# Matmuls of zeros at the start, hi and lo ahead of the additions in two MLPs, an earlier bias sum and a halved last eviction

## The chip, the cores and the metric

The kernel runs on one core of a Trainium2 chip. The metric is the device time of one execution in microseconds (us); of several runs the median counts. PE is the matmul engine, PEld its weight loads, DVE, ACT and POOL are the vector, scalar and GpSimd engines, SP issues most transfers.

## What is computed

```python
scores = (1.0 / S) * np.matmul(z, z.transpose(0, 2, 1))
attn = np.maximum(scores, 0.0) ** 2
x = u * np.matmul(attn, v)
h = x @ moe_w_in
x = np.maximum(0.01 * h, h) @ moe_w_out
r = np.maximum(x @ moe2_w_in, 0.0)
out = (s * (r * r) + b) @ moe2_w_out
```

There are 2 batches of S = 3008 tokens, 256 channels, a `z` of 64 channels, and 2048 hidden channels in each MLP. `u`, `z` and the result are handed over transposed.

## The kernel before

**Precision.** A float32 operand is kept as two parts, `hi` (rounded to the fast fp32r type) and `lo` (what is left of it). A product takes three matmuls: hi with hi, hi weights with lo, lo weights with hi.

**Tokens.** They are cut into 12 tiles, 10 of 512 columns and 2 of 448. The attention goes tile by tile; the MLPs take the tiles in 6 pairs of equal width.

**Attention.** A tile has 12 units, each of two blocks of 128 keys. `scores` (from line 316) issues four matmuls into a PSUM tile `f` (two buffers), then on ACT the activation Relu (L326) and the square (L327), then `hi` on ACT or DVE by turns (L328) and `lo` on DVE (L334). The value matmuls (L349) of a unit follow two units later in PE's order. `split_v` (from line 111) makes hi and lo of three blocks of `v`: hi on ACT (L114), lo on DVE for the first batch (L116). `load_v` fetches `v` three groups ahead. What happens in which unit is put down in `hooks` by `at(step, fn)`; `sv` runs `split_v` of group g at step `g * VG // 2` with `VG = 3`, so for g = 0 in step 0, ahead of that step's scores on ACT. Weights, given as float64, are narrowed and split on the side during the attention.

**MLPs.** For a pair of tiles the first product of an MLP is made in 8 blocks of 256 hidden channels (`q` = 0 to 7), each by the scheme with seven products in place of eight on 2 by 2 blocks: 21 matmuls (L415) into three PSUM tiles `x[0]` to `x[2]`. A block has three steps. Step one makes three products, copies `x[0]` to `s1` on ACT (L635) and forms `u2` on DVE (L638). Step two adds a product to `x[0]`, which ACT activates straight into `c11`, and one to `x[1]`; DVE then adds `x[1]` and `x[2]` to `s1` for `c22` (L660, L661). Step three adds A22's product to `x[1]` and S4's to `x[2]`, so it overwrites what L660 and L661 have read; DVE makes `c21` and `c12` (L672, L674).

**Second product.** The results of a block are activated while the next block runs: `activate(0)` for the pair's first tile and `activate(1)` for the second, on ACT (L591 in the first MLP; L593 and the square L604 in the second). `spread` then makes `hi` (L613: on ACT in the first MLP, on DVE in the second) and `lo` (L614, DVE) and puts 12 matmuls of the second product (L434) into a queue. Each step ends with `step_chunk`, which issues 8 of the queue on PE, except the step numbered 4, where nothing is taken. Each engine works through its own list strictly in the order in which the program issues it. In the last block of a pair, and in blocks 0 and 6, operands of the next pair or of this one are split besides (L407 on ACT, L408 on DVE).

**Bias.** `b` times the column sums of the last weights is needed for the last evictions. `bias_columns`, called in block 4 of the second pair of the first MLP, adds the two halves of the sum on DVE (L469) and multiplies by ones on PE (L472).

**End.** An accumulator of the second MLP is evicted by ACT (L451, channels 0 to 127) or DVE (L455, channels 128 to 255), and SP sends it out.

Of the kernel before, what the change touches and what calls it, by code (L numbers as in the profile page):

```python
# [10 lines left out]
F32 = mybir.dt.float32  # L11
F32R = mybir.dt.float32r
I32 = mybir.dt.int32
U32 = mybir.dt.uint32
AF = mybir.ActivationFunctionType
ALU = mybir.AluOpType
P = 128
# [3 lines left out]
QT = 512  # L21

VG = 3
# [5 lines left out]
def relu2_attention__then__leaky_mlp__then__relu2_mlp_kernel(  # L29
# [25 lines left out]
    nc = tc.nc  # L55
# [45 lines left out]
    def load_v(bb, g):  # L101
        raw = raw_pool.tile([P, 4 * D], F32, tag="raw", name="raw_v")
        r3 = raw.rearrange("p (n d) -> p n d", n=4)
        r0, n = g * VG * P, VG if g < NG - 1 else VG - 1
        nc.sync.dma_start(out=r3[:, 0:n, :], in_=v[bb, r0:r0 + n * P, :].rearrange("(n p) d -> p n d", p=P))
        if n < VG:
            for hh in range(2):
                nc.sync.dma_start(out=r3[hh * HALF:(hh + 1) * HALF, n, :], in_=v[bb, r0 + n * P:S, :])
        raws[bb, g] = raw
# [310 lines left out]
    def queue_second(m, pr, q, ti, hi, lo):  # L420
        t = pr[ti]
        bb, c, n = tiles[t]
        if q == 0:
            acc_t[m, t] = [None, None, None]

        def one(dh, f, i):
            acc = acc_t[m, t]
            if acc[dh] is None:
                acc[dh] = ps_a.tile([P, QT], F32, tag="acc", name=f"acc{dh}")
            w = st["out", m, q // 2]  # L430
            o = f * D + dh * P
            wh, x = ((0, hi), (0, lo), (1, hi))[i]
            last = q == NQ - 1 and f == 1 and i == 2
            nc.tensor.matmul(  # L434
                acc[dh][:, :n], lhsT=w[:, q % 2, wh, o:o + P], rhs=x[:, f, :n],
                start=q == 0 and f == 0 and i == 0, stop=last,
            )
            if m == 1 and pr == pairs[-1] and q % 2 == 1 and ti == dh == f == 1 and i == 2:
                fetch_out(2, q // 2)
            if not last:  # L440
                return
            if dh == 0:
                acc[2] = xio.tile([P, 2, QT], F32, tag="xo", name="x_sb")
            y = acc[2][:, dh, :n]
            if m == 1:
                nc.scalar.copy(out=y, in_=acc[dh][:, :n])
                if dh == 1:
                    nc.sync.dma_start(out=x_d[2, t][:, :, :n], in_=acc[2][:, :, :n])
            else:
                if dh == 0:  # L450
                    nc.scalar.activation(  # L451
                        out=y, in_=acc[0][:, :n], func=AF.Identity, scale=s_sb[:, 0:1], bias=cb[:, 0:1]
                    )
                else:
                    nc.vector.tensor_scalar(  # L455
                        out=y, in0=acc[1][:, :n], scalar1=s_sb[:, 0:1], scalar2=cb[:, 1:2],
                        op0=ALU.mult, op1=ALU.add,
                    )
                nc.sync.dma_start(out=outT[dh * P:(dh + 1) * P, bb * S + c:bb * S + c + n], in_=y)
            if dh == 1:  # L460
                acc_t.pop((m, t))

        for dh in range(2):
            for f in range(2):
                for i in range(3):
                    queue.append(lambda dh=dh, f=f, i=i: one(dh, f, i))

    def bias_columns():
        nc.vector.tensor_tensor(out=wtot, in0=wsum[:, 0:D], in1=wsum[:, D:2 * D], op=ALU.add)  # L469
        f = ps_x.tile([P, QT], F32, tag="x", name="f")  # L470
        for dh in range(2):
            nc.tensor.matmul(f[:, 2 * dh:2 * dh + 2], lhsT=wtot[:, dh * P:(dh + 1) * P], rhs=ones, start=dh == 0, stop=True, skip_group_check=dh > 0)  # L472
        nc.vector.tensor_scalar_mul(out=cb, in0=f[:, 0:4].rearrange("p (d two) -> p d two", two=2)[:, :, 0], scalar1=b_sb[:, 0:1])
# [3 lines left out]
    def at(step, fn):  # L477
        hooks.setdefault(max(step, 0), []).append(fn)

    with tc.manual_schedule():  # L480
# [14 lines left out]
        zrs[2] = load_zk(0, 2)  # L495
        load_v(0, 1)
        load_v(0, 2)
        zr0 = zrs.pop(0)
        make_zk(0, 0, zr0)
        make_zq(0, zr0)  # L500
# [10 lines left out]
        for g in range(NG):  # L511
            def sv(g=g):
                split_v(0, g)
                if g + 3 < NG:
                    load_v(0, g + 3)
            at(g * VG // 2, sv)

        for bb in range(1, B):
            base = bb * TPB * UA
# [96 lines left out]

        def step_chunk():
            nonlocal chunk
            if chunk != 4:
                take(8)  # L620
            chunk += 1

        for m, pr, q in quads:
# [22 lines left out]
            if q == NQ - 1 and ahead:  # L646
                pair_split(*ahead, ORDER[2:3], nc.vector)
            activate(0)
            if before and before[0] == 1:
                activate(1)  # L650
            if q == 4 and ahead:
# [7 lines left out]
            product(x[1], m, pr, q, S3, "T3", False)  # L659
            nc.vector.tensor_tensor(out=c22, in0=x2, in1=s1, op=ALU.add)  # L660
            nc.vector.tensor_tensor(out=c22, in0=x3, in1=c22, op=ALU.add)  # L661
            spread(0)
            if before and before[0] == 2:
                activate(1)
            if q == NQ - 1 and ahead:
# [15 lines left out]
                fetch_in(2, q)  # L681
            step_chunk()
            before = (m, pr, q, cs)
            if m == 1 and pr == pairs[1] and q == 4:
                bias_columns()
        for ti in range(2):
# [39 lines left out]
```

## Time and profile before

| | |
|---|---|
| median of 3 runs | 1515.65 us (1515.13 to 1516.13) |
| the profiled execution's own time | 1514.35 us |
| its span, first to last instruction | 1512.4 us |
| PE busy | 1498.3 us, 99% of the span |
| DVE busy | 1089.8 us, 72% |
| ACT busy | 915.8 us, 61% |
| POOL busy | 191.8 us, 13% |

The rows further down come from the one profiled execution. A time at the start of a row is counted from the span's beginning. Matmuls overlap, so the busy time of one is longer than the distance to the next.

### The profile page before, as it was taken

How to read it: one execution, taken by the hardware profiler on the slowest of the kernel's cores; microseconds unless marked ns; L12 is line 12 of the kernel's file. 1: busy time of each engine (PE TensorE's matmuls, PEld its weight loads, DVE VectorE, ACT ScalarE, POOL GpSimd, SP SyncE). 2: the span in 40 equal slices, each digit the busy share in tenths (PEclk: the TensorE clock that was granted, in tenths of full speed). 3: DMA queues.
4: the chain of work that ended last, by engine and by line, in shares of the span. 5: the costliest groups of instructions: out<-in, count | busy, mean ns of one | idle time of the engine just before them, and what ended most of it. 6: DMA issues, size and time to landing. Idle time of an engine off the chain costs nothing.

```text
span 1512.4 us, 16921 instructions
## 1 busy us (share of the span) xinstructions
PE 1498.3 (99%) x6604; PEld 1237.7 (82%) x6604; DVE 1089.8 (72%) x1369; ACT 915.8 (61%) x1118; POOL 191.8 (13%) x136
## 2 busy tenths in 40 slices
PE   8999999999999999999999999999999999999998
PEld 6888889888888978878889888887777878888776
DVE  6888875899995566566666666667767777777866
ACT  7778878787887645545454545464545545454543
POOL 0332326434431400000000000000000000000000
PEclk9999999999999999999999999999999999999999
DMA  5243434344334620001010102341010101010000
GB/s 156 95 130 130 152 138 126 108 167 153 110 136 158 239 78 17 40 0 53 1 56 1 53 0 105 117 155 42 1 57 1 53 1 56 1 53 1 28 0 28
DMA packets 38831, 113.21 MB, mean 75 GB/s; under 512 B 4064, under 2 KB 13792, under 8 KB 36704
## 3 DMA queue, kind: packets, MB, share of 16 engines
q1 hardware_dynamic: 38528, 111.88, 21.5%
q8 instruction: 51, 0.84, 0.2%
q10 hardware_dynamic: 160, 0.26, 0.1%
q14 instruction: 28, 0.23, 0.0%
q0 software_dynamic: 64, 0.00, 0.0%
HBM read 70.58 MB, written 41.55 MB: 74 GB/s over the span
## 4 chain that ended last, share of the span: by engine, by line
PE 97%; DVE 2%; DMA 0%; ACT 0%; issue 0%; SPq 0%; DVEq 0%
PE acc L434 34%; PE x L415 30%; PE acc L349 25%; PE f L323 8%; DMA raw_v<-in_v_dram 0%; DVE lo L614 0%; DVE lo L334 0%; DVE c L660 0%; DVE hi L332 0%; DVE c L661 0%; ACT a L327 0%; ACT a L326 0%; DVE hi L613 0%; DVE hi L328 0%; SPq L261 0%
## 5 line engine op out<-in xcount | busy, mean ns | idle before, releaser
L415 PE MATMUL x<-top,stat_i 128*128 128x512 f32 (+1 forms) x2016 | 498.6, 386 | 0.8 <-DVE c L660 0.8
L434 PE MATMUL acc<-hi,stat_o 128*128 128x512 f32 (+1 forms) x1536 | 483.7, 386 | 0.0
L415 PEld LDWEIGHTS x<-top,stat_i 128*128 128x128 f32 x2016 | 378.2, 188 | 74.5 <-DVE c L660 1.2
L349 PE MATMUL acc<-hi,stat_v 128*128 128x512 f32 (+1 forms) x1152 | 373.1, 388 | 0.0
L434 PEld LDWEIGHTS acc<-hi,stat_o 128*128 128x128 f32 x1536 | 288.4, 188 | 53.7
L434 PE MATMUL acc<-lo,stat_o 128*128 128x512 f32 (+1 forms) x768 | 301.7, 393 | 0.2
L349 PEld LDWEIGHTS acc<-hi,stat_v 128*128 128x128 f32 x1152 | 217.1, 188 | 42.4 <-DVE hi L328 0.5
L635 ACT COPY a<-x 128x512 f32<-128x512 f32 (+1 forms) x96 | 55.6, 579 | 310.0 <-PE x L415 310.0
L614 DVE TENSOR_TENSOR lo<-c,hi 128x1024 fp32r<-128x1024 f32 (+1 forms) x192 | 230.0, 1198 | 3.3
L334 DVE TENSOR_TENSOR lo<-a,hi 128x1024 fp32r<-128x1024 f32 (+1 forms) x132 | 188.8, 1431 | 56.5 <-ACT hi L328 54.0
L660 DVE TENSOR_TENSOR c<-x,a 128x512 f32<-128x512 f32 (+1 forms) x96 | 65.3, 680 | 221.4 <-PE x L415 221.4
L349 PE MATMUL acc<-lo,stat_v 128*128 128x512 f32 (+1 forms) x552 | 213.8, 387 | 0.7 <-DVE lo L334 0.7
L326 ACT ACTIVATE a<-f 128x1024 f32<-128x1024 f32 (+1 forms) x144 | 145.4, 1010 | 82.3 <-PE f L323 81.1
L434 PEld LDWEIGHTS acc<-lo,stat_o 128*128 128x128 f32 x768 | 144.1, 188 | 44.7 <-DVE lo L614 18.7
L323 PE MATMUL f<-zq,zk 128*128 128x512 f32 (+1 forms) x576 | 156.7, 394 | 7.0 <-DVE zk L272 5.3
L327 ACT ACTIVATE a<-a 128x1024 f32<-128x1024 f32 (+1 forms) x144 | 150.4, 1044 | 4.6
L323 PEld LDWEIGHTS f<-zq,zk 128*128 128x128 f32 x576 | 109.5, 191 | 31.0 <-ACT zq L285 5.3
L349 PEld LDWEIGHTS acc<-lo,stat_v 128*128 128x128 f32 x552 | 104.0, 188 | 22.0 <-DVE lo L334 1.8
L638 DVE TENSOR_TENSOR a<-x,a 128x512 f32<-128x512 f32 (+1 forms) x96 | 65.2, 679 | 68.6 <-PE x L415 67.8
L604 ACT ACTIVATE c<-c 128x1024 f32<-128x1024 f32 (+1 forms) x96 | 100.3, 1045 | 3.0
L613 ACT CAST hi<-c 128x1024 fp32r<-128x1024 f32 (+1 forms) x96 | 94.9, 1027 | 0.0
L593 ACT ACTIVATE c<-c 128x512 f32<-128x512 f32 (+1 forms) x96 | 79.7, 830 | 1.9 <-DVE c L672 1.9
(65 smaller groups left out, 1114.9 us busy)
## 6 DMA issues: line engine op xcount, KB each, us to landing
in_d<-stage_i SPq DMA_DIRECT2D x16, 896.0 KB, 5.9
stat_i<-in_d SPq DMA_DIRECT2D x16, 896.0 KB, 5.2
x_in<-x_d SPq DMA_DIRECT2D x20, 512.0 KB, 4.3
raw_w<-in_w_in_dram SPq DMA_DIRECT2D x16, 512.0 KB, 4.6
raw_w<-in_w_out_dram SPq DMA_DIRECT2D x16, 512.0 KB, 4.1
out_d<-stage_o SPq DMA_DIRECT2D x8, 1024.0 KB, 6.6
stat_o<-out_d SPq DMA_DIRECT2D x8, 1024.0 KB, 6.4
raw_v<-in_v_dram SPq DMA_DIRECT2D x14, 384.0 KB, 3.7
```

Source lines behind the costliest of these rows:

```text
L323: nc.tensor.matmul(f[:, j, :n], lhsT=lhsT, rhs=zq[t][:, h, :n], start=h == 0, stop=h == 1)
L326: nc.scalar.activation(out=a, in_=f[:, :, :n], func=AF.Relu, scale=scale)
L327: nc.scalar.activation(out=a, in_=a, func=AF.Square)
L334: nc.vector.tensor_sub(out=lo, in0=a, in1=hi.bitcast(F32))
L349: nc.tensor.matmul(acc_t[t][dh][:, :n], lhsT=w[:, wh, o:o + P], rhs=x[:, blk % 2, :n], start=blk == 0 and i == 0, stop=half and i == n_i - 1,)
L415: nc.tensor.matmul(x[:, :n], lhsT=w[:, wh, left, :], rhs=r[:, xh, :n], start=first and i == 0, stop=i == 2, skip_group_check=not first,)
L434: nc.tensor.matmul(acc[dh][:, :n], lhsT=w[:, q % 2, wh, o:o + P], rhs=x[:, f, :n], start=q == 0 and f == 0 and i == 0, stop=last,)
L593: nc.scalar.activation(out=out, in_=x, func=AF.Relu)
L604: nc.scalar.activation(out=c, in_=c, func=AF.Square)
L613: (nc.scalar.copy if m == 1 else nc.vector.tensor_copy)(out=hi, in_=c)
L614: nc.vector.tensor_sub(out=lo, in0=c, in1=hi.bitcast(F32))
L660: nc.vector.tensor_tensor(out=c22, in0=x2, in1=s1, op=ALU.add)
```

## The change

Six places change.

1. DVE clears a tile `zeros` at the start, and PE multiplies it with itself into a PSUM tile that nobody reads: 9 matmuls ahead of the first scores, 4 ahead of the scores of unit 2.
2. `split_v` and the `load_v` behind it run one unit later in the first batch.
3. In the MLPs `spread(0)` moves from behind the additions L660 and L661 of step two to step one, right behind `activate(0)`. In the first MLP it thereby also stands ahead of `activate(1)`.
4. `step_chunk` now leaves out the steps 3 and 4, so that PE's order of matmuls stays as it was.
5. The addition for `wtot` moves from block 4 to the end of block 2 of the same pair.
6. The eviction of the last accumulator is cut in two halves of 256 columns: the second on DVE, sent by SP, the first on ACT, sent from ACT's queue.

```diff
@@ in queue_second @@
                 else:
+
+                    half = n // 2 if t == pairs[-1][1] else 0
                     nc.vector.tensor_scalar(
-                        out=y, in0=acc[1][:, :n], scalar1=s_sb[:, 0:1], scalar2=cb[:, 1:2],
+                        out=y[:, half:], in0=acc[1][:, half:n], scalar1=s_sb[:, 0:1], scalar2=cb[:, 1:2],
                         op0=ALU.mult, op1=ALU.add,
                     )
-                nc.sync.dma_start(out=outT[dh * P:(dh + 1) * P, bb * S + c:bb * S + c + n], in_=y)
+                    if half:
+                        nc.scalar.activation(
+                            out=y[:, :half], in_=acc[1][:, :half], func=AF.Identity, scale=s_sb[:, 0:1], bias=cb[:, 1:2]
+                        )
+                        nc.scalar.dma_start(out=outT[P:D, bb * S + c:bb * S + c + half], in_=y[:, :half])
+                        nc.sync.dma_start(out=outT[P:D, bb * S + c + half:bb * S + c + n], in_=y[:, half:])
+                if dh == 0 or t != pairs[-1][1]:
+                    nc.sync.dma_start(out=outT[dh * P:(dh + 1) * P, bb * S + c:bb * S + c + n], in_=y)
...
     def bias_columns():
-        nc.vector.tensor_tensor(out=wtot, in0=wsum[:, 0:D], in1=wsum[:, D:2 * D], op=ALU.add)
...
         load_v(0, 2)
+
+        zeros = parts.tile([P, 2, QT], F32R, tag="hi", name="zeros")
+        nc.vector.memset(zeros[:, 0].bitcast(F32), 0.0)
+        idle = ps_a.tile([P, QT], F32, tag="acc", name="idle")
+
+        def keep_busy(k):
+            for _ in range(k):
+                nc.tensor.matmul(idle, lhsT=zeros[:, 0, 0:P], rhs=zeros[:, 0], start=True, stop=True)
+
+        keep_busy(9)
+        at(2, lambda: keep_busy(4))
...
-            at(g * VG // 2, sv)
+            at(g * VG // 2 + 1, sv)
...
         def step_chunk():
             nonlocal chunk
-            if chunk != 4:
+            if chunk not in (3, 4):
                 take(8)
...
             activate(0)
+            spread(0)
             if before and before[0] == 1:
                 activate(1)
...
             nc.vector.tensor_tensor(out=c22, in0=x3, in1=c22, op=ALU.add)
-            spread(0)
...
             before = (m, pr, q, cs)
+            if m == 1 and pr == pairs[1] and q == 2:
+                nc.vector.tensor_tensor(out=wtot, in0=wsum[:, 0:D], in1=wsum[:, D:2 * D], op=ALU.add)
             if m == 1 and pr == pairs[1] and q == 4:
                 bias_columns()
```

DVE in the last block of the second MLP's first pair. The names are those of the lines above; in the changed kernel L613 and L614 are L632 and L633, L638 is L657, L660 and L661 are L680 and L681, L672 is L691. Before:

```order
L638 TENSOR_TENSOR a<-x_8465,a 128x512
L408 TENSOR_TENSOR top<-tsum,top 128x512
L660 TENSOR_TENSOR c<-x_8465,a 128x512
L661 TENSOR_TENSOR c<-x_8466,c 128x512
L613 CAST hi<-c 128x1024
L614 TENSOR_TENSOR lo<-c,hi 128x1024
L408 TENSOR_TENSOR top<-x_in,top 128x512
L672 TENSOR_TENSOR c<-x_8465,a 128x512
```

And now:

```order
L657 TENSOR_TENSOR a<-x_8481,a 128x512
L408 TENSOR_TENSOR top<-tsum,top 128x512
L632 CAST hi<-c 128x1024
L633 TENSOR_TENSOR lo<-c,hi 128x1024
L680 TENSOR_TENSOR c<-x_8481,a 128x512
L681 TENSOR_TENSOR c<-x_8482,c 128x512
L408 TENSOR_TENSOR top<-x_in,top 128x512
L691 TENSOR_TENSOR c<-x_8481,a 128x512
```

The cast and the subtraction have moved ahead of the two additions; the rest keeps its place.

ACT at the start of the program, before (`zq` is the first operand of the scores, `stat_v` the split of `v`):

```order
L285 CAST zq<-zr 128x512
L114 CAST stat_v<-raw_v 128x768
L326 ACTIVATE a<-f 128x1024
L327 ACTIVATE a<-a 128x1024
L114 CAST stat_v<-raw_v 128x768
L326 ACTIVATE a<-f 128x1024
L327 ACTIVATE a<-a 128x1024
L328 CAST hi<-a 128x1024
```

And now:

```order
L285 CAST zq<-zr 128x512
L326 ACTIVATE a<-f 128x1024
L327 ACTIVATE a<-a 128x1024
L114 CAST stat_v<-raw_v 128x768
L326 ACTIVATE a<-f 128x1024
L327 ACTIVATE a<-a 128x1024
L328 CAST hi<-a 128x1024
L114 CAST stat_v<-raw_v 128x768
```

The copy of `v` now stands behind the activation and the square of the same unit's scores.

ACT at the end of the changed program, with what each instruction waits for in brackets (`acc_11190` is the last accumulator, which DVE's half reads too):

```order
L612 ACTIVATE c<-c 128x1024 [waits DVE_49]
L623 ACTIVATE c<-c 128x1024 [waits Activation_49]
L451 ACTIVATE x_sb<-acc_11135,cb,s_sb 128x512 [waits DMAHW3_49,DMAHW2_49,PE_49]
L451 ACTIVATE x_sb<-acc_11172,cb,s_sb 128x512 [waits DMAHW5_49,DMAHW4_49,PE_49]
L462 ACTIVATE x_sb<-acc_11190,cb,s_sb 128x256 [waits DVE_49]
L465 DMA out_dram<-x_sb 128x256 [waits Activation_49]
```

The last two rows are new: ACT's half, which waits for DVE, and the transfer from ACT's queue.

## Rows read from the trace of the kernel before

**Rows 1.** The chain that ended last, shares of the span by engine.

```profile
PE 97%; DVE 2%; DMA 0%; ACT 0%; issue 0%; SPq 0%; DVEq 0%
```

**Rows 2.** Timeline of PE: first products of pairs (start us, us, engine, line, operation).

```profile
684.22 0.62 PE L415 MATMUL x<-top,stat_i 128*128 128x512 f32 x2
...
921.56 0.63 PE L415 MATMUL x<-top,stat_i 128*128 128x512 f32 x2
...
1171.40 0.62 PE L415 MATMUL x<-top,stat_i 128*128 128x512 f32 x2
...
1414.61 0.63 PE L415 MATMUL x<-top,stat_i 128*128 128x512 f32 x2
```

**Rows 3.** Timeline of one block of the second MLP (in brackets idle before, and releaser).

```profile
1026.40 1.06 ACT L604 ACTIVATE c<-c 128x1024 f32<-128x1024 f32 x1
...
1029.79 0.69 DVE L660 TENSOR_TENSOR c<-x,a 128x512 f32<-128x512 f32 x1 [3.09 <-PE x L415]
...
1031.12 0.68 DVE L613 CAST hi<-c 128x1024 fp32r<-128x1024 f32 x1
...
1031.40 1.52 PE L415 MATMUL x<-top,stat_i 128*128 128x512 f32 x6
1031.84 1.23 DVE L614 TENSOR_TENSOR lo<-c,hi 128x1024 fp32r<-128x1024 f32 x1
1032.76 0.39 PE L434 MATMUL acc<-hi,stat_o 128*128 128x512 f32 x1
...
1033.12 0.50 PE L434 MATMUL acc<-lo,stat_o 128*128 128x512 f32 x1
```

**Rows 4.** Timeline around the bias sum.

```profile
650.98 0.39 PE L434 MATMUL acc<-lo,stat_o 128*128 128x512 f32 x1
...
652.89 0.61 PE L472 MATMUL f<-ones,wtot 128*128 128x2 f32 x4 [1.53 <-DVE wtot L469]
```

**Rows 5.** Timeline of the second MLP's first pair, block 6, then block 7.

```profile
1069.35 1.06 ACT L604 ACTIVATE c<-c 128x1024 f32<-128x1024 f32 x1
...
1073.30 1.52 PE L415 MATMUL x<-top,stat_i 128*128 128x512 f32 x6
...
1080.19 1.06 ACT L604 ACTIVATE c<-c 128x1024 f32<-128x1024 f32 x1
...
1083.79 1.52 PE L415 MATMUL x<-top,stat_i 128*128 128x512 f32 x6
```

**Rows 6.** Timeline of one block of the first MLP.

```profile
550.23 1.58 ACT L591 ACTIVATE c<-c 128x512 f32<-128x512 f32 x2
...
554.10 1.99 ACT L613 CAST hi<-c 128x1024 fp32r<-128x1024 f32 x2
...
554.28 0.69 DVE L660 TENSOR_TENSOR c<-x,a 128x512 f32<-128x512 f32 x1 [3.09 <-PE x L415]
```

**Rows 7.** Who PE waited for, whole span (us in total, times, longest).

```profile
PE x L415 <- DVE c L660: 0.8, 1, 0.8
```

**Rows 8.** Timeline of the beginning.

```profile
0.81 0.06 DVE L491 MEMSET ones<- 128x2 f32 x1 [0.81 <-PEq L713]
...
5.29 3.99 PE L323 MATMUL f<-zq,zk 128*128 128x512 f32 x8 [5.29 <-DVE zk L272]
...
9.14 0.83 ACT L114 CAST stat_v<-raw_v 128x768 fp32r<-128x768 f32 x1 [4.54 <-DMA raw_v<-in_v_dram]
...
10.01 0.96 DVE L116 TENSOR_TENSOR stat_v<-raw_v,stat_v 128x768 fp32r<-128x768 f32 x1 [1.13 <-ACT stat_v L114]
...
10.95 2.08 PE L323 MATMUL f<-zq,zk 128*128 128x512 f32 x4 [1.67 <-ACT a L326]
...
18.04 1.09 PE L323 MATMUL f<-zq,zk 128*128 128x512 f32 x4
```

**Rows 9.** The last eviction (timeline), then groups by line and form (busy, mean ns).

```profile
1508.42 0.81 DVE L455 TENSOR_SCALAR x_sb<-acc,s_sb,cb 128x512 f32<-128x512 f32 x1 [1.91 <-PE acc L434]
...
L455 DVE TENSOR_SCALAR x_sb<-acc,s_sb,cb 128x448 f32<-128x448 f32 x2 | 1.5, 740 | 0.7 <-PE acc L434 0.7
```

## Prediction

> **What bounds the kernel now.** I read the chain of work that ended last first, then who PE waited for, then the timeline of single stretches. The chain lies on PE for 97% of the span [rows 1], so a change is worth exactly what it takes out of PE's order or out of PE's holes; ACT and DVE count only where PE stands waiting for them. The lists of instructions say that PE runs the same matmuls in the same order as before, with 13 matmuls of zeros ahead of or between the first scores. So the question is which holes close, and whether new ones open.
>
> There are four kinds of hole. First, many small ones in the second MLP. Pairs 2, 3 and 4 of the first MLP take from 684.22 to 921.56, 237.34 us; the same pairs of the second MLP, same matmuls, take from 1171.40 to 1414.61, 243.21 us [rows 2]. That is 5.87 us in 24 blocks, 0.245 a block. Where it sits is seen in one block [rows 3]: the first `hi` matmul of the third step starts at 1032.76 and the next, which reads `lo`, at 1033.12. That is 0.36 where neighbours in a steady run stand 0.23 apart (six start and drain in 1.52), and it takes 0.50 where its neighbour takes 0.39: 0.13 of waiting and 0.11 for weights that could not be loaded ahead, 0.24. The subtraction that writes `lo` starts at 1031.84 and takes 1.23, so it ends at 1033.07, and PE goes on 0.05 later. DVE does hi and lo only behind the addition L660, which begins at 1029.79 after 3.09 us of idling for PE, although the square that hi reads ended at 1026.40 + 1.06 = 1027.46. The second hole is the bias sum: the last matmul ahead of it starts at 650.98, the first one of L472 at 652.89, 1.53 us of it idling for `wtot` [rows 4]. The third is the beginning, the fourth the last eviction; both below.
>
> **The second MLP, hi and lo ahead of the additions.** After the change DVE may begin hi at 1027.5; 0.68 and 1.23 [rows 3] (0.7 and 1.15 from start to start) put its end at 1029.4, before L660's operands come at 1029.79. So the additions do not move and lo is there 3.7 us early: the hole closes. 47 blocks have it (48, less the first, whose hi and lo belong to the first MLP): 47 × 0.245 = **11.5 us**. When the last block drains the same wait stands once more, some **0.3**.
>
> Not every block has that much room. In the last block of a pair that has a follower (5 of them) ACT first splits an operand of the next pair, the square starts at 1080.19 and ends at 1081.25 [rows 5]. Then hi and lo hold DVE until about 1083.15, L660 ends at 1083.85, and PE, whose product A22 overwrites what L660 reads, is free at 1083.79: a new wait of 0.06 + 0.05, and the 0.11 for weights. So 0.2 stands in place of 0.245: 5 × 0.2 = **-1.0**. In blocks 0 and 6, where two operands are split, the square starts at 1069.35 and L660 would end near 1073.05, against 1073.30 for PE [rows 5]: just in time, 0; at most 0.2 in each of 11 such blocks, 2.2, is kept for the range.
>
> **The first MLP.** There hi is ACT's. It now follows the first of two activations that begin at 550.23 and take 1.58 together [rows 6]; 0.55 for the short one and 1.0 for hi (two take 1.99) end it at 551.8, lo at 553.0. L660 begins at 554.28, so 1.2 us are left, and nothing moves: 0. One exception is block 1 of the first pair, where no queued matmuls cover the products and PE waits for L660 already [rows 7]: lo in front of it makes that wait 0.55 longer, and the lo wait behind it (0.2) goes: **-0.3**.
>
> **The bias sum.** `wtot` is made two blocks earlier, behind the last lo of a block, where DVE's next work, L638, waits for PE's products; it hides there, and without that cover would cost what it takes, at most 0.7 (an addition on twice the columns), once. PE goes on after 0.23 instead of 1.91: **1.7**. The four short matmuls stay.
>
> **The beginning.** PE finishes the eight scores of units 0 and 1 at 9.28 and stands until 10.95, because ACT has v's copy ahead of the first activation, and that copy waits 4.54 us for its transfer, until 9.14 [rows 8]. PE then waits for lo and v again (v's subtraction alone takes 0.96 from 10.01) and starts the scores of unit 3 at 18.04. After the change ACT takes the first activation as soon as four scores are done, by half of the 3.99 about 7.4; I take 7.6, since nine matmuls of zeros come first. They can begin once DVE has cleared the tile, about 1.5 (its first operation starts at 0.81 [rows 8]; on twice the columns hi takes 0.68), and at half rate (four take 2.08 at 10.95 and 1.09 at 18.04 [rows 8], that is 1.2 and 2.4 GHz) they take 4.1, until 5.6, against 5.29 when the first operands were ready. Then: activation 1.03 and square 1.06, 9.7; hi 0.7, lo 1.15, 11.6; v's subtraction L116 0.96, 12.6, while v's copy runs on ACT from 9.7. The third value matmul needs that; ten more at 0.23 follow with one late weight load, 15.0, and the scores of unit 3 begin there instead of at 18.04: **3.0**. That takes full rate by 12.6. If PE stays at half until 17, the ten take 4.4 and 1.0 is left. If it rises before the first scores, the chain starts 0.6 sooner, 3.6. In the trace PE worked from 5.29 to 9.28 and again from 10.95 at half rate, with a hole between, and had the full rate by 18.04; with the zeros it works from 1.5 to about 9 without a pause, so I take the full rate. The Trainium skill (TensorE: Matmul & The Clock Gate, Part 1) says the engine starts throttled, activity releases it, and the moment differs from run to run; no row here shows a second run's moment. Loads of v go out a unit later, but so do the splits that need them; 0.
>
> **The last eviction.** L455 on 512 columns starts at 1508.42 and takes 0.81 [rows 9]. It becomes a half on DVE and a half on ACT. From 448 to 512 columns DVE's operation grows by 0.068, so 256 should take 0.54; ACT's half has no row; I put it at the same. Side by side this would give back 0.25. But ACT's half stands in the list with a wait for DVE, and both read one PSUM bank. One after the other they take 1.13 with 0.05 between, 0.32 more, and the last transfer leaves from ACT. The row of before has no second reader to show it, so the bounds are +0.25 and -0.6; I take **-0.4**, because the wait is written in the order. The Trainium skill (PSUM — Partial Sum Buffer, PSUM bank collisions raise a hardware error) says that two engines must not be in one bank and quadrant at once, reads included. By that rule the halves cannot overlap and this part loses; without it the sum would be 0.65 us better.
>
> **Sum.** 11.5 + 0.3 - 1.0 - 0.3 + 1.7 + 3.0 - 0.4 = 14.8 us. The profiled execution took 1514.35 (its span is 1512.4), which gives 1499.5; the median of the runs is 1.3 higher, which gives 1500.8. I say **1500.0**, between the two.
>
> **Rivals.**
> *DVE's order turns against it (slower).* Hi and lo now stand ahead of L660, and DVE waits for ACT with nothing that could pass. In a plain block lo ends at 1029.4, and PE notices only when L660 begins after 1030.55 (0.69 of its own and 0.16 for a late weight load before 1031.40). So this decides at 1.15 us of delay of the square or of lo; beyond that PE pays one to one. If both came 1.5 us later than I reckon, 0.35 in each of some 90 blocks, 31 us, would make 1500 + 31 = 1531. For it: the last blocks already go over that point by my own sum. Against it: in plain blocks the square starts from the same result as before and DVE idles 3.09 us at this place. 3%.
> *The wait is replaced.* If hi or lo comes early but half of the 0.245 was something else (a slower read, say), or the eleven tight blocks and five last ones lose 0.3 each, 4 to 6 us stay: 1504 to 1506. For it: the margin in blocks 0 and 6 is 0.25 and the weights' 0.11 comes off it. Against it: the 0.24 of the one wait already is the whole difference of 0.245. 14%.
> *The beginning gives little.* The zeros delay the scores or the rate stays at half until 17: 1 us instead of 3, 1502. 12%.
> *It does not do what it says.* PE's rows would have to wait for something else throughout, and the time would stay at 1514 to 1516. 2%.
>
> **How the numbers follow.** My forecast holds with 69% and spans 1497 to 1503: 0.6 at the beginning, 0.65 at the end, 1 for the last blocks, and 1 either way for what buffers that lie elsewhere may do to PE's spacing. Reaching to the replaced wait gives 1496.5 to 1505. About 3 us, 0.2%, is what a measurement of this kernel can tell from no change. Faster by more: 0.95; within it: 0.02; slower: 0.03.
>
> **What would show it.** In the second MLP 0.23 from hi to lo, and pairs 2 to 4 in about 238; a wait of about 0.1 to 0.2 for L660 in last blocks only; four L472 matmuls without idling; scores of unit 3 near 15; ACT's last half after DVE's. It is wrong if PE shows waits for L660 or for lo in most blocks, or if the first MLP's 237.3 us grow.

## The result, and the profile after

The changed kernel takes 1498.89 us, the median of 5 runs (1498.40 to 1500.27); before stands at 1515.65 beside it (5 runs, 1514.98 to 1516.13). The ratio is 0.9892, with a 95% interval of 0.9877 to 0.9906: 16.8 us, or 1.1%, faster. Forecast were 1500.0, within 1496.5 to 1505.0. The profiled execution took 1498.4 with a span of 1496.6, against 1512.4 before, so the trace has to account for 15.8 us.

The chain that ended last still lies on PE [rows 1]. Shares of the span by engine:

```profile
PE 98%; DVE 1%; ACT 1%; issue 0%; DMA 0%; DVEq 0%; ACTq 0%
```

First products of pairs 2 and 5 on PE, first in the first MLP, then in the second (start us, us, engine, line, operation; pairs and blocks are counted from 0, as in the prediction), to be read beside [rows 2]:

```profile
679.22 0.84 PE L415 MATMUL x<-top,stat_i 128*128 128x512 f32 x3
...
916.56 0.86 PE L415 MATMUL x<-top,stat_i 128*128 128x512 f32 x3
...
1163.03 0.84 PE L415 MATMUL x<-top,stat_i 128*128 128x512 f32 x3
...
1401.08 0.63 PE L415 MATMUL x<-top,stat_i 128*128 128x512 f32 x2
```

Pairs 2 to 4 of the first MLP take 916.56 - 679.22 = 237.34 us, as before to the hundredth. The same pairs of the second MLP take 1401.08 - 1163.03 = 238.05, where they took 243.21. One of its blocks shows why (block 2 of pair 0, timeline, in brackets the idle time before and its releaser; compare [rows 3]):

```profile
1021.12 1.06 ACT L623 ACTIVATE c<-c 128x1024 f32<-128x1024 f32 x1
...
1022.21 0.69 DVE L632 CAST hi<-c 128x1024 fp32r<-128x1024 f32 x1 [0.80 <-ACT c L623]
...
1022.94 1.22 DVE L633 TENSOR_TENSOR lo<-c,hi 128x1024 fp32r<-128x1024 f32 x1
1022.94 1.52 PE L415 MATMUL x<-top,stat_i 128*128 128x512 f32 x6
...
1024.50 0.69 DVE L680 TENSOR_TENSOR c<-x,a 128x512 f32<-128x512 f32 x1 [0.34 <-PE x L415]
...
1027.48 0.39 PE L434 MATMUL acc<-hi,stat_o 128*128 128x512 f32 x1
...
1027.70 0.39 PE L434 MATMUL acc<-lo,stat_o 128*128 128x512 f32 x1
```

`lo` ends at 1024.16, before the addition L680 may begin, and DVE's old wait for PE ahead of that addition has shrunk from 3.09 to 0.34 us: it is filled with hi and lo. The matmul that reads `lo` starts 0.22 behind its neighbour instead of 0.36, and takes 0.39 instead of 0.50.

Three more places. The bias sum goes on without a hole [rows 4], though DVE's addition is not shorter:

```profile
647.77 0.40 PE L434 MATMUL acc<-lo,stat_o 128*128 128x512 f32 x1
...
648.00 0.50 PE L480 MATMUL f<-ones,wtot 128*128 128x2 f32 x4
```

At the beginning [rows 8] the first activation stands ahead of v's copy, and the scores of unit 3 begin at 14.36 instead of 18.04:

```profile
1.49 3.84 PE L513 MATMUL idle<-zeros 128*128 128x512 f32 x9 [1.49 <-DVE zeros L508]
...
5.29 0.47 PE L323 MATMUL f<-zq,zk 128*128 128x512 f32 x1
5.92 1.89 PE L323 MATMUL f<-zq,zk 128*128 128x512 f32 x7 [0.16 <-DVE zq L287]
...
6.92 1.03 ACT L326 ACTIVATE a<-f 128x1024 f32<-128x1024 f32 x1 [2.32 <-PE f L323]
...
8.94 0.82 ACT L114 CAST stat_v<-raw_v 128x768 fp32r<-128x768 f32 x1
...
14.36 0.85 PE L323 MATMUL f<-zq,zk 128*128 128x512 f32 x3
```

Seven of the first eight scores now take 1.89 us, where all eight took 3.99: they run at full rate already (2.4 GHz, the upper of the two levels; 512 columns then start 0.23 apart, and 0.43 apart at the lower one, 1.2 GHz). At the end [rows 9] the two halves stand one behind the other, ACT's half behind 1.16 us of idling for DVE's:

```profile
1492.52 0.54 DVE L457 TENSOR_SCALAR x_sb<-acc,s_sb,cb 128x256 f32<-128x256 f32 x1 [1.91 <-PE acc L434]
...
1493.10 0.56 ACT L462 ACTIVATE x_sb<-acc,cb,s_sb 128x256 f32<-128x256 f32 x1 [1.16 <-DVE x_sb L457]
```

Taken from the starts of first products of blocks (L415) and of the last eviction, the 15.8 us of span come from these places:

| place | before | after | difference | forecast |
|---|---|---|---|---|
| span's start to the first block of the first MLP | 521.41 | 517.73 | -3.68 | -3.0 |
| block 1 of the first MLP | 7.95 | 8.42 | +0.47 | +0.3 |
| block with the bias sum | 12.42 | 10.64 | -1.79 | -1.7 |
| second MLP, first block's start to last block's start | 484.62 | 474.27 | -10.35 | -10.3 |
| last block's start to the last eviction's | 20.11 | 19.55 | -0.55 | -0.5 |
| last eviction's start to the end | 4.0 | 4.1 | +0.1 | +0.4 |

The forecasts of rows four and five are the prediction's 47 blocks, split where the last begins: 46 x 0.245 less 1.0, and 0.245 + 0.3.

### The profile page after: what moved, and what is told of

The parts are those of the page before. It is cut to its first block, busy times and chain, and to the rows that moved or that the text cites. A ratio compares the mean times of both kernels' runs of the same rounds, so it can differ in the third digit from the quotient of the medians.

```text
span 1496.6 us, 16905 instructions
## 1 busy us (share of the span) xinstructions
PE 1487.8 (99%) x6617; PEld 1241.5 (83%) x6617; DVE 1107.5 (74%) x1370; ACT 918.9 (61%) x1119; POOL 191.7 (13%) x136
## 4 chain that ended last, share of the span: by engine, by line
PE 98%; DVE 1%; ACT 1%; issue 0%; DMA 0%; DVEq 0%; ACTq 0%
PE acc L434 34%; PE x L415 30%; PE acc L349 25%; PE f L323 8%; DMA zr<-in_zT_dram 0%; DVE lo L334 0%; DVE hi L332 0%; ACT a L327 0%; ACT a L326 0%; DVE hi L328 0%; DVE lo L633 0%; DVE raw_w L149 0%; ACT hi L632 0%; DVE stat_v L116 0%; ACT hi L328 0%
## 5 line engine op out<-in xcount | busy, mean ns | idle before, releaser
L415 PE MATMUL x<-top,stat_i 128*128 128x512 f32 (+1 forms) x2016 | 499.5, 387 | 1.5 <-DVE c L680 1.5
L415 PEld LDWEIGHTS x<-top,stat_i 128*128 128x128 f32 x2016 | 377.3, 188 | 77.0 <-DVE c L680 3.6
L434 PE MATMUL acc<-lo,stat_o 128*128 128x512 f32 (+1 forms) x768 | 296.1, 386 | 0.0
L633 DVE TENSOR_TENSOR lo<-c,hi 128x1024 fp32r<-128x1024 f32 (+1 forms) x192 | 230.6, 1201 | 39.2 <-ACT hi L632 35.9
L657 DVE TENSOR_TENSOR a<-x,a 128x512 f32<-128x512 f32 (+1 forms) x96 | 65.3, 680 | 87.8 <-PE x L415 87.4
L691 DVE TENSOR_TENSOR c<-x,a 128x512 f32<-128x512 f32 (+1 forms) x96 | 65.2, 679 | 71.9 <-PE x L415 71.9
L632 ACT CAST hi<-c 128x1024 fp32r<-128x1024 f32 (+1 forms) x96 | 98.7, 1028 | 1.5
L632 DVE CAST hi<-c 128x1024 fp32r<-128x1024 f32 (+1 forms) x96 | 65.0, 678 | 35.2 <-ACT c L623 35.2
```

The lines of the kernel that those rows point to most:

```text
L415: nc.tensor.matmul(x[:, :n], lhsT=w[:, wh, left, :], rhs=r[:, xh, :n], start=first and i == 0, stop=i == 2, skip_group_check=not first,)
L434: nc.tensor.matmul(acc[dh][:, :n], lhsT=w[:, q % 2, wh, o:o + P], rhs=x[:, f, :n], start=q == 0 and f == 0 and i == 0, stop=last,)
L632: (nc.scalar.copy if m == 1 else nc.vector.tensor_copy)(out=hi, in_=c)
L633: nc.vector.tensor_sub(out=lo, in0=c, in1=hi.bitcast(F32))
L657: nc.vector.tensor_tensor(out=u2, in0=x2, in1=s1, op=ALU.add)
L691: nc.vector.tensor_tensor(out=c21, in0=x2, in1=s1, op=ALU.add)
```

## Experiments

Diffs are against the changed kernel. Names in the text are those of the changed kernel too; where a row of an experiment has another line number, it is told. The kernel before, run again beside them, took 1516.41 us beside e1 to e4 (8 runs), 1517.60 beside e5 to e8 (one run) and 1515.26 beside e9 to e12 (7 runs). These medians lie up to 2 us apart, so small differences are read from the traces, block by block, and not from totals; e2 to e8 have one run each.

**e1_spread_back: only the order of hi and lo undone.**

```diff
-            if chunk not in (3, 4):
+            if chunk != 4:
...
             activate(0)
-            spread(0)
...
             nc.vector.tensor_tensor(out=c22, in0=x3, in1=c22, op=ALU.add)
+            spread(0)
```

> The changed kernel with hi and lo of the first tile back behind the additions in both MLPs; PE's order of matmuls is the same. Lateness of lo (my theory): the second MLP's pairs 2 to 4, from 238.05 us in the changed kernel, return to 243.2; block 1 of the first pair goes from 8.42 back to 7.95; in all about 10.9 - 0.5 = 10.4 us slower than the changed kernel, 1509.3. Rival, that the hole closed because buffers lie elsewhere or because of the earlier parts of the change: the pairs stay near 238 and the time near 1499.

It took 1510.24 us (5 runs, 1509.47 to 1511.41), ratio to before 0.9958 (0.9944 to 0.9972). In its trace pairs 2 to 4 of the second MLP are back at 243.19 us and block 1 of the first MLP at 7.95. Its span is 10.7 us longer than that of the changed kernel, and the ratios to before differ by 10.0 us. So the order alone is worth 10 to 11 of the 16.8 us, and the rest of the change 5 to 6. That is the theory's size (10.4), and the rival, other places of buffers or the rest of the change, would have left the pairs near 238.

**e2_no_zeros: the matmuls of zeros and the clearing of their tile left out; the output is the same.**

```diff
...
-        keep_busy(9)
-        at(2, lambda: keep_busy(4))
```

> The changed kernel without the matmuls of zeros and without their tile; v's split stays a unit later. The first block of the first MLP starts at 517.73 in the changed kernel and at 521.41 in the kernel before. If the zeros only bring full rate to the first scores: they end near 7.6 in place of 6.9, and the first block starts 0.7 later, near 518.4 (full rate by 12.6 without them). Rival, that without them PE stays at half rate to about 17: ten value matmuls at 0.43, 2.6 later, near 520.3.

One run: 1499.54 us. The first MLP begins at 518.77, 1.04 later than with the change, of which 0.3 are a later transfer of the first operand. That is near the theory and far from the rival's 520.3, but one run is not enough, as the spread further down shows.

**e3_v_stays: v split at the old place, zeros kept.**

```diff
-            at(g * VG // 2 + 1, sv)
+            at(g * VG // 2, sv)
```

> The changed kernel with the split of v in its old unit, so that ACT's copy of v, which waits for its transfer until 9.1, stands ahead of the first activation again; the zeros stay. My theory: the third scores wait for ACT until 10.95 as before, but PE is at full rate, so only the ten value matmuls at the end are quicker; the scores of unit 3 start near 16.9 (18.04 before, 14.36 in the changed kernel), and the first block of the first MLP near 520.3. Rival, that the rate is what gave the 3.7 us: near 518.

One run: 1503.51 us, and a miss on both sides. The first MLP begins at 522.84, later than in the kernel before. PE has the full rate from 6.09 on, then idles 2.40 us for the activation behind v's copy, and from 12.91 to 19.74 its matmuls start 0.43 apart again; the granted clock of 13 to 17 us is 0.50, which is 1.2 GHz. The scores behind the hole:

```profile
11.24 1.21 PE L323 MATMUL f<-zq,zk 128*128 128x512 f32 x4 [2.40 <-ACT a L326]
```

The full rate came early with the zeros, and it was lost again behind the hole that v's copy leaves. The last runs test whether that was chance.

**e4_bias_back: the addition for the bias back in block 4.**

```diff
     def bias_columns():
+        nc.vector.tensor_tensor(out=wtot, in0=wsum[:, 0:D], in1=wsum[:, D:2 * D], op=ALU.add)
...
-            if m == 1 and pr == pairs[1] and q == 2:
-                nc.vector.tensor_tensor(out=wtot, in0=wsum[:, 0:D], in1=wsum[:, D:2 * D], op=ALU.add)
```

> The changed kernel with the addition for wtot back in front of the multiplication by ones. DVE reaches it behind lo and a subtraction, as before: block 4 of the second pair takes 12.4 us in place of 10.64, 1.8 slower in all. Rival, that DVE with its new order reaches it earlier by the time of lo, 1.2: 11.2.

One run: 1501.19 us, with a beginning that was 1.3 later for its transfers. The block takes 11.94, between the two expectations. PE's matmuls around the sum (L481 is L480 there):

```profile
649.06 0.39 PE L434 MATMUL acc<-lo,stat_o 128*128 128x512 f32 x1
650.49 0.61 PE L481 MATMUL f<-ones,wtot 128*128 128x2 f32 x4 [1.04 <-DVE wtot L478]
```

PE idles 1.04, not 1.53 as in [rows 4]. In the kernel before, DVE works without a pause here from the first tile's `lo` to `wtot`, and the second tile's `lo` starts 0.30 ahead of PE's last matmul; with the first tile's `lo` done earlier, it starts 0.78 ahead of it, at 648.28. So the moved subtraction without the moved addition brings 0.49 of the 1.79 us that this block gained. The reverse case stands in e1, where hi and lo are at their old place and the addition is moved: the block takes 10.64 there too, and nothing idles ahead of the sum:

```profile
647.54 0.40 PE L434 MATMUL acc<-lo,stat_o 128*128 128x512 f32 x1
647.77 0.50 PE L480 MATMUL f<-ones,wtot 128*128 128x2 f32 x4
```

So the moved addition alone brings the whole 1.79, and the moved subtraction adds nothing to it.

**e5_second_only: hi and lo ahead of the additions in the second MLP alone.**

```diff
-            if chunk not in (3, 4):
+            if chunk != 4:
...
-            spread(0)
+            if before and before[0] == 2:
+                spread(0)
...
             nc.vector.tensor_tensor(out=c22, in0=x3, in1=c22, op=ALU.add)
+            if before and before[0] == 1:
+                spread(0)
```

> The same computation; hi and lo of the first token tile stand ahead of the additions in the second MLP alone, in the first MLP behind them as before the change. Theory: the first MLP gained nothing from the move and lost in one place, block 1 of its first pair, which took 7.948 us before and 8.421 with the change, because PE waits there for L680 behind lo. So block 1 comes back to 7.95, pairs 2 to 4 of the first MLP stay at 237.34, those of the second at 238.05, and the span is 0.5 shorter than with the change but for what the beginning does. Rival: the 0.47 came from the eight queued matmuls that the change takes out of that block's middle, not from lo; then, as they are put back here too, this run alone shows the same, but pairs 2 to 4 of the second MLP or its first block would show a new wait for lo of 0.2 us.

One run: 1498.6 us, with a beginning 0.41 later, so that the total hides the gain. Block 1 of the first MLP takes 7.96 instead of 8.42, all its other blocks are equal to 0.02 us, and the second MLP keeps its gain (474.33 us to its last block's start, for 474.27). So in the first MLP the move brought nothing and cost 0.46. The rival, that the eight matmuls taken elsewhere are the cause, is not excluded by this run alone, since they come back with it; the trace of the changed kernel speaks for the theory: PE waits 1.47 us there for L680, which starts at 531.36, right behind the `lo` ahead of it (from 530.22, 1.22 long); in e5, with `lo` behind L680, PE waits 0.78, as before the change.

**e6_split_behind: in last blocks the split of the third operand behind hi and lo.**

```diff
-            if q == NQ - 1 and ahead:
-                pair_split(*ahead, ORDER[2:3], nc.vector)
             activate(0)
             spread(0)
+            if q == NQ - 1 and ahead:
+                pair_split(*ahead, ORDER[2:3], nc.vector)
```

> The same computation; in the last block of a pair the split of the next pair's third operand is placed behind hi and lo instead of ahead of them, on ACT and DVE. Theory: last blocks did not gain because the split makes the square late, hi and lo then hold DVE beyond PE's need, and a wait for L680 stands in place of the old one for lo. With the split behind, last blocks of the second MLP fall from 10.48 to between 10.20 and 10.27 us, like plain ones, 1.0 to 1.3 us in all, and the waits of PE's weight loads for L680 (3.6 us over six) nearly go. Rival: last blocks are held by something else (the reading of new operands, the first activations of ACT), and stay at 10.48; or the split, late now, makes the first block of the next pair wait, and what is won is lost there.

One run: 1497.54 us, as the theory has it. The block of [rows 5] that starts at 1070.14 in the changed kernel:

```profile
1074.65 0.70 DVE L632 CAST hi<-c 128x1024 fp32r<-128x1024 f32 x1 [0.93 <-ACT c L623]
...
1076.53 0.68 DVE L680 TENSOR_TENSOR c<-x,a 128x512 f32<-128x512 f32 x1
...
1077.27 0.53 PEld L415 LDWEIGHTS x<-top,stat_i 128*128 128x128 f32 x3 [0.37 <-DVE c L680]
1077.27 1.68 PE L415 MATMUL x<-top,stat_i 128*128 128x512 f32 x6
```

The same block with the split behind, 0.34 us later in its span:

```profile
1073.60 0.69 DVE L632 CAST hi<-c 128x1024 fp32r<-128x1024 f32 x1 [0.80 <-ACT c L623]
...
1076.07 0.68 DVE L680 TENSOR_TENSOR c<-x,a 128x512 f32<-128x512 f32 x1
...
1077.28 1.32 PEld L415 LDWEIGHTS x<-top,stat_i 128*128 128x128 f32 x6
1077.51 1.52 PE L415 MATMUL x<-top,stat_i 128*128 128x512 f32 x6
```

`hi` starts 1.39 us earlier in the block, weights are loaded ahead again, and the six matmuls take 1.52 instead of 1.68. The last blocks of pairs 0 to 4 fall from 10.48, 10.53, 10.43, 9.50 and 10.48 to 10.20, 10.27, 10.20, 9.28 and 10.20: 1.27 us. The second MLP as a whole is 1.22 shorter up to its last block, so next to nothing is lost at the blocks behind.

**e7_hi_twice and e8_hi_three_more: hi copied once, and three times, more than needed, so that DVE comes late to L680.**

```diff
             hi, lo = split_parts(c, tiles[pr[0]][2])
+            if m == 2 and ti == 0:
+                for _ in range(1):
+                    nc.vector.tensor_copy(out=hi, in_=c)
```

(3 for 1 in the second.)

> The same computation, but in the second MLP hi of the first token tile is copied once more than needed, so that DVE comes to L680 about 0.7 us later in each of its blocks. Theory: a plain block has 1.15 us of room ahead of L680 before PE notices, so blocks 2 and 3 of pairs stay at 10.20 and 10.27 us; blocks without that room (the last ones by 0.7, blocks 6 and 0 by 0.4 to 0.7, blocks 1, 4 and 5 between 0 and 0.7) pay, 8 to 18 us in all. Rival, that hi and lo at the head of DVE's order leave no room at all: all blocks grow by 0.7, 33 us in all, 1530 or above.

> The same computation, but in the second MLP hi of the first token tile is copied three times more than needed, so that DVE comes to L680 about 2.1 us later in each block. Theory: beyond 1.15 us of delay PE pays one to one, so blocks 2 and 3, untouched by one copy, now grow by 2.1 - 1.15 = about 1.0 us, to 11.2; with 1.0 to 2.1 in the others the whole comes to 1545 to 1575. Rival one: no room from the start, 2.1 in each block, 1595 or above. Rival two: DVE's order does not reach PE at this place, blocks 2 and 3 stay at 10.2, and the time stays under 1520.

With one copy, 0.72 us, the time is 1513.49. Blocks 2 and 3 of pairs stay at 10.20 and 10.27, but for 0.15 in one block of pair 3, whose tiles have 448 columns; last blocks of 512 columns go to 11.1 to 11.3, most blocks 6 and 0 to 10.8 to 10.9; blocks 4 and 5 grow by about 0.2 and blocks 1 by 0 to 0.6; in the last pair, which splits nothing for a follower, nothing grows from block 2 on. The whole is 13.3 us in the second MLP, inside the 8 to 18 expected. So the rival's "no room at all" falls, and so does "room everywhere". With three, 2.15 us (L634 is the extra copy, L683 is L680), blocks 2 and 3 go to 11.27, 1.07 more. PE's waits in the whole span:

```profile
PE x L415 <- DVE c L683: 61.4, 48, 2.1
```

The theory's 2.15 - 1.15 = 1.0 for plain blocks is thus right, but its total is not: 1591.04 lies above 1575. The excess is in blocks 7 and 0 and some blocks 6, which pay about 1.6 us more than the delay explains (a block's time less its time with one copy, less 1.43 for two more). The windows of pair 0's block 6 (us, busy time and count by engine, then granted clock, DMA share, GB/s):

```profile
1074.05:1075.80 1.75, 0.01 (x1) 0.00 (x0) 1.72 (x2) 0.19 (x1) 0.00 (x0) 1.00 0.00 0
1075.82:1077.30 1.48, 1.48 (x6) 1.15 (x7) 1.15 (x2) 0.00 (x0) 0.00 (x0) 1.00 0.00 0
1077.30:1080.30 3.00, 3.00 (x8) 2.28 (x8) 2.73 (x4) 0.00 (x0) 0.00 (x0) 0.51 0.00 0
1080.75:1082.90 2.15, 2.15 (x11) 1.77 (x10) 0.49 (x1) 0.59 (x1) 0.00 (x0) 0.99 0.00 0
```

PE stood for 1.77 us, about the first window, worked on at full rate, and then had the lower of the two levels for over 3 us. Eleven blocks show it; 11 x 1.6 = 17.6, and 1591.0 - 17.6 = 1573 is inside the theory's range. So, by this estimate from block times, the theory's sum holds but for the clock.

**e9_best to e12_best_old_start: three parts corrected, and the beginning in its four forms.** e9 is e5 and e6 together, with the last eviction whole again:

```diff
-                    half = n // 2 if t == pairs[-1][1] else 0
+                    half = 0
...
-                if dh == 0 or t != pairs[-1][1]:
-                    nc.sync.dma_start(out=outT[dh * P:(dh + 1) * P, bb * S + c:bb * S + c + n], in_=y)
+                nc.sync.dma_start(out=outT[dh * P:(dh + 1) * P, bb * S + c:bb * S + c + n], in_=y)
```

The others are e9 without zeros (as e2), with v at its old place (as e3), and with both.

> The same computation; three parts of the change corrected by what the runs show: hi and lo ahead of the additions in the second MLP alone (as in the run with the second MLP only), the split of the third operand behind them in last blocks, and the last eviction whole again, on DVE, with one transfer. Theory: 0.46 and 1.18 us from the first two, as each gave alone, and 0.1 from the last (the last eviction's start to the end of the span: 4.10 with halves, 4.01 whole), so 1498.9 - 1.7 = 1497.2. Rival: halves save after all, since they leave the work of the last transfer smaller; then the end takes 4.1 or more and the sum is 1497.4 or above.

> As the run with three parts corrected, without the matmuls of zeros and the clearing of their tile. Theory: zeros let the clock rise earlier and bring 0.4 to 1.0 us (one look without them had the first MLP begin at 518.77, seven looks with them between 517.73 and 519.52), so 0.4 to 1.0 us slower than with them. Rival: their part lies within what the landing of transfers varies from run to run: within 0.3 us.

> As the run with three parts corrected, with zeros, but v split at the old place, ahead of the activation of the first scores. Theory: the hole of over 2 us that ACT leaves there comes behind the rise of the clock and sends it back to half rate, so the beginning is later than with neither part: first MLP at 522 to 523, against 518.4 on the mean, 4 to 5 us slower. Rival: the fall of the rate in the one look was that run's chance; then the clock stays at full rate, the first MLP begins near 520.3, and it is 2 us slower.

> As the run with three parts corrected, but with the beginning as before the change: no zeros, and v split at the old place. Theory: the first MLP begins near 521.4 as before, against 518.4 on the mean, so 3.0 us slower than with the new beginning, and faster than with zeros and v at the old place by 1 us or more. Rival: most of what the new beginning brings needs no zeros and no move but comes from how transfers land in a run: within 1 us.

All four ran on one chip beside the same runs of before (median 1515.26, 7 runs); each has 4 runs:

| | v split a unit on | v at the old place |
|---|---|---|
| with zeros | e9: 1497.17 (1496.83 to 1497.73) | e11: 1501.31 (1501.19 to 1501.92) |
| without | e10: 1497.67 (1497.37 to 1498.27) | e12: 1501.26 (1500.88 to 1501.74) |

e9 has a ratio to before of 0.9879 (0.9862 to 0.9895). It is the fastest version: its slowest run (1497.73) is below the fastest of the changed kernel (1498.40), though on another chip, on which the median of before was 0.4 lower, and the intervals of the two ratios overlap; the traces show the gain in its places, block 1 of the first MLP at 7.95 and last blocks at 10.20 and 10.27. The theory had 1497.2. In its trace the last eviction starts at 1491.32 and the span ends at 1495.3, 4.0 later, where the halves needed 4.1; the rival, that halves save after all, falls.

The column "v a unit on" is 3.6 to 4.1 us faster than the other; the rows differ by 0.5 with the move, in overlapping ranges, and by nothing without it. So the move carries the beginning, and zeros help little on top of it and not at all alone. Of the expectations, e11 came out as its theory had it (first MLP at 522.15, 4.1 slower), and e12 missed: it is 4.1 slower than e9 where 3.0 were expected, and equals e11 where it was to be 1 us or more faster.

The 0.5 of the zeros can't be told from the rival's 0.3 by these times, but the traces tell more. From the first score to the first score of unit 3 it takes 9.07 to 9.08 us in four profiles with zeros (changed kernel, e6, e8, e9) and 9.75 and 9.74 in the two without (e2, e10); other profiles with zeros have a late transfer or a fall of the rate on the way. So zeros bring about 0.7 on top of the move, and part of it is hidden by when the first transfers land, which moves the first score itself between 5.29 and 5.81.

Where the move brings its part, e10 against e12 shows:

```profile
5.44 4.70 PE L323 MATMUL f<-zq,zk 128*128 128x512 f32 x12 [5.44 <-DVE zk L272]
10.75 0.47 PE L349 MATMUL acc<-hi,stat_v 128*128 128x512 f32 x1 [0.61 <-DVE hi L328]
```

```profile
11.14 2.08 PE L323 MATMUL f<-zq,zk 128*128 128x512 f32 x4 [1.72 <-ACT a L326]
13.02 0.74 PE L349 MATMUL acc<-hi,stat_v 128*128 128x512 f32 x1
```

The first value matmul starts 2.27 earlier, since ACT's first activation no longer stands behind v's copy, and the scores of unit 3 start 3.13 earlier (15.18 for 18.31), so the other 0.86 is the full rate on the way from the one to the other.

Granted clock and work of 13 to 15 us, in e11 and then in e9:

```profile
13.00:15.00 2.00, 1.54 (x4) 0.86 (x4) 1.77 (x2) 1.94 (x3) 0.00 (x0) 0.50 0.52 144
```

```profile
13.00:15.00 2.00, 2.00 (x10) 1.62 (x10) 1.56 (x2) 2.00 (x3) 0.00 (x0) 1.00 0.65 172
```

And the scores of unit 2 ahead of it, in e11:

```profile
10.88 1.27 PE L323 MATMUL f<-zq,zk 128*128 128x512 f32 x4 [2.19 <-ACT a L326]
```

The fall of the rate behind the hole, seen once in e3, repeats in e11: the hole of 2.19 us comes behind work at full rate, and then the clock is at 0.50. In e12, with a hole of 1.72 us and no zeros, matmuls start 0.43 apart until 17.37 as before. In e10, with neither zeros nor hole, they start 0.23 apart from 8.78 on, and in e2 from about 9.5. In e10 this is ahead of the place where the hole stood: up to there e10 and e12 have the same scores at the same times, and the rate rose in one and not in the other. Why it rose so early there, no run shows.

## Why the prediction was right, point by point

**Where the time is.** PE sets the end, and its matmuls are the same in the same order; e1 and the table of places show no difference that isn't a hole of PE closed or opened. Right.

**The second MLP, 11.5 - 1.0.** Measured -10.35 to the last block's start, against -10.3. The reading of one block in [rows 3], 0.13 of waiting and 0.11 for late weights, holds: both went together. The 0.245 is a mean: plain blocks of 512 columns went from 10.47 to 10.20 and from 10.53 to 10.27, most of those of 448 columns from 9.45 to 9.29. The rival "the wait is replaced" is refuted for plain blocks and true where the prediction put it: last blocks stayed at 10.48, and the new wait for L680 there is what e6 takes away, 1.27 in five blocks where the prediction had 1.0. Blocks 6 and 0, "0, at most 0.2 each", lost 0.05 or less.

**Room ahead of L680, 1.15 us.** The prediction's decision point for the slower case. e7 and e8 measured it: 0.72 of delay costs plain blocks nothing, 2.15 costs 1.07, so the point lies near 1.1. That rival was not far away: one copy of 0.7 us more on DVE costs 13.3 us, more than the move brought.

**The first MLP, 0 and -0.3.** Right in place, low in size: block 1 lost 0.47. The wait for L680 grew from 0.78 to 1.47, that is by 0.7 and not by 0.55, and 0.2 of the old wait for `lo` went.

**The bias, 1.7.** Measured 1.79, and for the stated cause: the moved addition alone brings all of it (e1). The prediction did not see that the moved subtraction alone would bring 0.49 of it (e4).

**The beginning, 3.0: the term with the largest miss, 0.7 low, and the step whose reason fell in part.** In size the 3.7 are the prediction's other case, "if it rises before the first scores, 3.6": the scores began where they did before, 5.29, but at full rate, so the activation came at 6.92 instead of the assumed 7.6. The reason was worse than the number. The prediction let the full rate come from the zeros ("with the zeros it works from 1.5 to about 9 without a pause"). e9 to e12 and e2 show otherwise: with v's copy moved, the rate rises without zeros too, at 8.7 and 9.5 us, ahead of the 12.6 that the prediction's 3.0 needed. The move alone is worth those 3.0 (12.75 from the first score to unit 3's scores before, 9.75 in e2), and the zeros the 0.7 on top. Zeros with the old hole (e11) win nothing. So the prediction had the chain of work on ACT and DVE right, but the full rate that it also took would have come early without the zeros too, and that 3.0 is near the measured 3.7 is in part luck. The Trainium skill (TensorE: Matmul & The Clock Gate, Part 1) says that the moment at which the rate rises differs from run to run. The trace agrees: in eight profiles with the change's beginning the spacing fell from 0.43 to 0.23 us at different moments between 4.6 and 7.0 us, and in one of them (e7) the rate fell back for a while.

**The last eviction, -0.4.** The order decided, as the prediction took it: the halves are serial, and 0.54 + 0.04 + 0.56 = 1.14 stand in place of 0.81, the forecast 0.32 more. But only 0.1 was lost: from the last operation's end to the span's end it is 3.0 us with a half as the last transfer and 3.2 with the whole (e9), and this 0.2 had no term. The Trainium skill (PSUM — Partial Sum Buffer, PSUM bank collisions raise a hardware error) says that two engines must not be in one bank and quadrant at once. ACT's wait of 1.16 us for DVE agrees with an order made by that rule; no run here shows what the halves would take side by side.

**The sum.** 14.8 forecast, 15.8 in the trace. The misses are 0.7 at the beginning, 0.3 at the end, and 0.2 or less elsewhere.

## What to carry to other kernels

Where an engine idles for another and then does work that was ready before, moving that work into the idle time cost nothing here as long as it ended before the wait did: subtract the two times from one block's timeline, and do it again for every kind of block, because those with extra work have no such room. Where a start-up is slow, look for the transfer that an engine waits for ahead of work that could already run, before adding work that only keeps TensorE busy. Cutting the last operation in two for two engines can gain only if both work at once; here the second waited for the first.

## What the runs showed of the hardware

The granted clock fell to half in the middle of dense work, behind holes that seem short. In e8 PE had stood for 1.77 us and lost the full rate 1.5 us later, for over 3 us, at a cost of 1.6. In block 6 of pair 4 a hole of the same length had no such consequence. The matmuls behind the two holes, and the 5 us behind the second one:

```profile
1075.82 1.69 PE L415 MATMUL x<-top,stat_i 128*128 128x512 f32 x6 [1.77 <-DVE c L683]
...
1463.29 1.67 PE L415 MATMUL x<-top,stat_i 128*128 128x512 f32 x6 [1.77 <-DVE c L683]
```

```profile
1463.30:1468.30 5.00, 5.00 (x22) 4.06 (x23) 3.92 (x6) 0.59 (x1) 0.00 (x0) 1.00 0.00 0
```

So the length of the hole alone doesn't decide. In e3 and e11 the holes were 2.40 and 2.19 us. In e7 there were only gaps of 0.4 to 0.5 us at 10 to 12 us, around the first values, in a beginning that is the change's own, while the changed kernel has gaps of 0.3 to 0.7 there and e4 one of 1.0, without a fall. What brought the fall in e7 stays open:

```profile
13.00:15.00 2.00, 2.00 (x7) 1.51 (x6) 1.56 (x2) 2.00 (x3) 0.00 (x0) 0.50 0.69 231
```

Its first MLP began at 519.52. In the seven other profiles with this beginning it began between 517.73 and 519.04, partly by when the first transfers land. So the new beginning is not safe from this fall. The slowest of the changed kernel's five runs, 1500.27, is also the one with the lowest mean granted clock, 0.998; that fits such a fall, but no trace of that run shows where it was.

The column of the granted clock can't be read at the beginning alone. In e12 it stands at 1.00 for 13 to 15 us, while two value matmuls take 1.05 us where they take 0.62 at full rate:

```profile
13.00:15.00 2.00, 1.53 (x4) 0.93 (x4) 2.00 (x2) 1.94 (x3) 0.00 (x0) 1.00 0.46 160
```

```profile
14.81 1.05 PE L349 MATMUL acc<-hi,stat_v 128*128 128x512 f32 x2
```

The Trainium skill (TensorE: Matmul & The Clock Gate, Part 1) warns that a trace's clock events aren't to be fully trusted. This row agrees: until the first rise the distance of matmuls shows the rate, and the column doesn't.
